# A fused Fourier mix on one core: the order of all work given as an explicit list, with the even row pairs moved and the first transform's sums dealt out anew

**Chip, cores, metric.** The kernel runs on one core of one Trainium2 chip. The metric is the device time of one execution in microseconds (us). PE is TensorE, PEld its weight loads, DVE is VectorE, ACT is ScalarE, POOL is GpSimd, SP is the engine whose queue issues nearly all transfers.

## The reference

```python
# x: 1 x 2048 x 1024 bf16; w_r, w_i: 2048 x 513; gate_w: 1024
g = sigmoid((x * gate_w).sum(-1, keepdims=True))
a = irfft2(rfft2(x) * (A_w_r + 1j * A_w_i))     # -> bf16
b = irfft2(rfft2(x) * (B_w_r + 1j * B_w_i))     # -> bf16, the same x
return g * a + (1 - g) * b
```

The transforms are computed as matrix products. The kernel has five parts, and the text uses these names for them.

- **Head.** The first transform, F1, of the 16 row groups of x. Each row gives two results, an even one and an odd one (e = 0 and 1), and each of the 32 results needs one sum and one difference of halves, a *row fold*. A row fold is done by DVE (from PSUM, after ACT has copied one half out), by POOL (from SBUF, after the whole has been copied out), or inside the matmuls (a *sum*, with twice the matmuls and then one plain copy).
- **Steps 0 to 15.** Each takes the second transform (F2, F3), multiplies by the weights W (two DVE *products*, c1 and c2, per step), does the first inverse transform, and writes a block of 512 KB to DRAM. Steps 0 to 7 belong to the even half, 8 to 15 to the odd half. In steps 0 to 7, POOL also computes three tiny *edge terms*, which the inverse matmuls need.
- **Read-backs.** The blocks return in another layout, eight row pairs for each half. An odd row pair needs the last block.
- **Row pairs.** The second inverse transform with the gate, for eight even pairs and eight odd ones. The odd ones combine both halves into the output.
- **Gate.** Two sigmoids on ACT and the gate weights on DVE. Every row pair needs its gate weights first.

## The kernel before

Its order is the order of the calls. POOL had five double folds (10 of the 32 row folds), DVE 20, and two were summed in PE.

```python
    def f1_pool(i, e, k=None):          # two rows: copied whole to SBUF by ACT, folded by POOL
        at = wk.tile([P, 2, 2, 256], F32, name="at4", tag=f"p{(i + e) % 2}", bufs=3)
        ...
        av = at[:].rearrange("p s h (a c) -> p h s a c", c=4)
        fold(nc.gpsimd, 2 * i, e, av[:, 0], av[:, 1])          # an add and a subtract
    ...
    def cmul(n, r, tts=((0, 2),)):      # one product: 128x2048 bf16, both inputs in SBUF
        ...
            nc.vector.tensor_tensor(o, xr, wv, ALU.mult)
    ...
    Wh = const.tile([P, NU, 2, 2, 4], F32, name="wh")
    for b, op in ((0, ALU.add), (2, ALU.subtract)):
        for t in range(2):
            nc.gpsimd.tensor_tensor(Wh[:, :, :, t, b:b + 2], ws[:, 0, :, :, t, b:b + 2], ws[:, 1, :, :, t, b:b + 2], op)   # waits for the small load ws
    gwz = const.tile([P, 8, 32], BF16, name="gwz")
    nc.gpsimd.memset(gwz[:], 0.0)                                                         # ACT's first work waits for this
    ...
    f1_fold(0, 0, 0)()                  # the head
    f1_pool(0, 1)
    f1_fold(2, 0, 1)()
    f1_pool(1, 1)
    ...                                 # f1_pool(4, 0), f1_pool(2, 1), f1_pool(3, 1) among DVE folds
    for n in range(3, 16):
        mid(n)                          # f3(n-1), cmul_2(n-2), load_w(n+3), f2(n), cmul_1(n-1), i1(n-2); for n = 11..14 two even read-backs
    f3(15); cmul_2(14); gate_z(0, 0); cmul_1(15); cmul_2(15)     # (one call to a line)
    i1(14, "ADA"); gate_weights(0); i1(15, "ADA")
    for s0 in range(0, NS1, 2):
        read_back(1, s0)
    i2(0, 0); gate_z(1, 0); gate_weights(1); i2(0, 1); i3_even(0, 1)
    stage = [(0, 1), (0, 2), (0, 3), (0, 4), (1, 0), (0, 5), (1, 1), (0, 6), (1, 2), (0, 7), (1, 3), ...]   # (0, v) even, (1, v) odd
```

## Time and profile before

| | |
|---|---|
| median, range of 3 runs | 125.18 us, 123.96 to 125.72 |
| span of the profiled run | 124.5 us (that run took 126.41 us) |
| busy: PE, DVE, ACT, POOL | 83%, 74%, 73%, 34% |
| POOL's folds | 10.28 to 22.68 us |
| step 3's first product | 36.5 us |
| last product of step 15 | 77.7 us |
| last block issued, landed | 82.25, 89.40 us |

In the list of instructions in order of time, the columns are the start (us), the time taken (us), the engine, the source line, the operation, what it writes and reads, how many, and in brackets how long the engine had been idle and who released it. POOL's last folds and first edge terms, in the kernel before:

```profile
20.18 2.50 POOL L257 TENSOR_TENSOR y<-at_403 128x512 bf16<-128x512 f32 x2
22.63 0.67 POOL L415 TENSOR_TENSOR e_529<-X_157,wh 128x16 f32<-128x16 bf16 x1
```

POOL is nearly through with its folds (22.68 us) when the first product needs DVE (22.08 us). The two products of step 3:

```profile
36.52 1.23 DVE L407 TENSOR_TENSOR p_779<-X_158,w_119 128x2048 bf16<-128x2048 bf16 x1 [0.48 <-ACT X_158 L384]
...
38.34 1.21 DVE L407 TENSOR_TENSOR p_780<-X_158,w_119 128x2048 bf16<-128x2048 bf16 x1
```

A run is labelled slow when it is over 1.5% above the fastest of the same kernel, and the profiled run of the kernel before was such a run.

### The profile page before, as it was taken

The page shows a single profiled execution, that of the slowest core. Times are in us where ns is not written, and L with a number is a line of the kernel's source. Part 1 is how long each engine was busy: PE and PEld are TensorE (multiplying, and loading weights), DVE is VectorE, ACT ScalarE, POOL GpSimd, SP SyncE. Part 2 cuts the span into 40 slices and gives each one's busy share as a digit, 9 for nine tenths or more (in the row PEclk, how much of TensorE's full clock was granted, in tenths as well). Part 3 has the DMA queues.
Part 4 walks back from the last instruction along what each step waited for, and adds up shares of the span by engine and source line. Part 5 has one row for each costly group of instructions (what it writes and reads, how often), then busy time and mean ns, then how long its engine had stood idle before and what let it go on. Part 6 is the DMA issues. An engine that isn't in the chain of part 4 may idle for free.

```text
span 124.5 us, 3756 instructions
## 1 busy us (share of the span) xinstructions
PE 103.7 (83%) x1556; PEld 70.9 (57%) x1558; DVE 92.5 (74%) x134; ACT 90.7 (73%) x147; POOL 42.6 (34%) x52
## 2 busy tenths in 40 slices
PE   6938999993999889988998994679919999999930
PEld 2538997872444444554454452379818999766500
DVE  0118995989689999699899899844960667778980
ACT  3029787976499999899999997699813988833510
POOL 0036999950124453400000000000000079997080
PEclk9999999999599999999999999999995999999998
DMA  2999999981929999979999999999199950407984
GB/s 93 361 396 404 384 408 411 392 328 68 290 89 308 328 294 366 316 243 239 341 402 402 413 403 412 397 399 371 55 311 419 411 213 5 169 5 286 396 335 163
DMA packets 18289, 37.41 MB, mean 301 GB/s; under 512 B 1756, under 2 KB 10848, under 8 KB 18272
## 3 DMA queue, kind: packets, MB, share of 16 engines
q1 hardware_dynamic: 17664, 36.90, 80.7%
q10 hardware_dynamic: 576, 0.26, 0.8%
q8 instruction: 12, 0.20, 0.6%
q14 instruction: 5, 0.04, 0.1%
q0 software_dynamic: 32, 0.01, 0.0%
HBM read 24.58 MB, written 12.58 MB: 299 GB/s over the span
## 4 chain that ended last, share of the span: by engine, by line
PE 29%; DVE 19%; DMA 13%; POOL 13%; ACT 13%; issue 9%; ACTq 1%; DVEq 1%; POOLq 0%
POOL y L257 10%; PE ps L454 9%; DMA h_152<-rl 6%; ACT rl L252 5%; DMA ws<-in_ws_dram 5%; DVE rl L252 4%; PE ia L436 4%; DMA ro<-h_152 3%; ACT T L252 2%; DVE y L257 2%; PE ps L353 2%; ACT X_158 L384 2%; ACT X_157 L384 2%; PE ps L313 2%; PE pt_2282 L499 1%
## 5 line engine op out<-in xcount | busy, mean ns | idle before, releaser
L465 POOL TENSOR_TENSOR ot<-re,y 128x1024 bf16<-128x1024 f32 x6 | 14.0, 2369 | 48.3 <-DVE y L465 48.3
L252 ACT CAST y<-ps 128x512 bf16<-128x512 f32 x32 | 17.5, 604 | 8.0 <-PE ps L454 8.0
L252 ACT CAST rl<-ia 128x1024 bf16<-128x1024 f32 x16 | 16.5, 1033 | 3.5 <-PE ib L436 3.4
L248 PEld LDWEIGHTS <-re 128*128 128x128 bf16 x240 | 13.6, 98 | 4.0 <-DMA re<-in_x_dram 2.2
L353 PE MATMUL ps<-fd,y 128*128 128x256 bf16 x112 | 15.4, 277 | 0.6 <-DVE e_991 L371 0.4
L252 ACT CAST T<-ps 128x512 bf16<-128x512 f32 x23 | 13.4, 635 | 0.1
L436 PEld LDWEIGHTS <-wi 32*64 32x64 bf16 x512 | 6.9, 106 | 10.4 <-issue 5.9
L353 PEld LDWEIGHTS <-y 128*128 128x128 bf16 x112 | 9.8, 98 | 4.9 <-issue 3.9
L252 DVE CAST rl<-ib 128x512 bf16<-128x512 f32 x16 | 10.9, 684 | 1.8 <-PE ib L436 1.6
L454 PE MATMUL ps<-ea,ro 128*128 128x128 bf16 x64 | 8.8, 230 | 2.8 <-DMA ro<-h_152 2.8
L454 PEld LDWEIGHTS <-ro 128*128 128x128 bf16 x128 | 8.5, 103 | 3.9 <-DMA ro<-h_152 3.1
L382 PEld LDWEIGHTS <-wf 64*64 64x64 bf16 x180 | 5.2, 108 | 9.6 <-issue 5.6
L252 ACT CAST rl<-ib 128x512 bf16<-128x512 f32 x16 | 9.8, 614 | 0.0
L475 PEld LDWEIGHTS <-y 128*128 128x128 bf16 x88 | 8.5, 102 | 1.1
L454 PE MATMUL ps<-eb,ro 128*128 128x128 bf16 x64 | 8.8, 230 | 0.0
L454 PEld LDWEIGHTS <-re 128*128 128x128 bf16 x128 | 7.8, 98 | 1.4 <-issue 1.2
L454 PE MATMUL ps<-ea,re 128*128 128x128 bf16 x64 | 8.1, 219 | 0.6 <-ACT y L252 0.6
L454 PE MATMUL ps<-eb,re 128*128 128x128 bf16 x64 | 8.1, 219 | 0.0
L248 PE MATMUL ps<-f_89,re 128*128 128x128 bf16 x96 | 6.4, 219 | 1.6 <-ACT at_180 L280 1.6
L465 DVE TENSOR_TENSOR re<-pt_2008,e_2017 128x512 f32<-128x512 f32 x2 | 1.3, 686 | 5.0 <-ACT e_2017 L479 5.0
L252 DVE CAST T<-ps 128x512 bf16<-128x512 f32 x5 | 3.4, 685 | 0.9 <-PE ps L353 0.9
L234 ACT ACTIVATE junk<-gwz 128x8 f32<-128x8 bf16 x1 | 0.2, 209 | 5.1 <-POOL gwz L231 5.1
(294 smaller groups left out, 265.2 us busy)
## 6 DMA issues: line engine op xcount, KB each, us to landing
h_151<-rl SPq DMA_DIRECT2D x8, 512.0 KB, 4.9
h_152<-rl SPq DMA_DIRECT2D x8, 512.0 KB, 8.8
re<-h_151 SPq DMA_DIRECT2D x8, 512.0 KB, 9.9
ro<-h_152 SPq DMA_DIRECT2D x8, 512.0 KB, 6.5
re<-in_x_dram SPq DMA_DIRECT2D x6, 512.0 KB, 7.1
out_dram<-ot SPq DMA_DIRECT2D x6, 512.0 KB, 2.7
ro<-in_we_dram SPq DMA_DIRECT2D x4, 512.0 KB, 7.2
ro<-in_wo_dram SPq DMA_DIRECT2D x4, 512.0 KB, 6.9
```

Source lines behind the costliest of these rows:

```text
L248: nc.tensor.matmul(o[:, q * 128:(q + 1) * 128], lhsT=x[:, s1, h * 512 + q * 128:h * 512 + (q + 1) * 128], rhs=F1[:, h * e, :], start=(h == ...
L252: (nc.scalar.copy if eng == "A" else nc.vector.tensor_copy)(out=out, in_=in_)
L257: eng.tensor_tensor(o, av, bv, op)
L313: nc.tensor.matmul(ps[32 * j:32 * j + 32], lhsT=gwz[:, k, :], rhs=y[:, k // 4, k % 4, 8 * j:8 * j + 8, :, :].rearrange("p t s c -> p (t s ...
L353: nc.tensor.matmul(ps[:, q // 2 * 256:q // 2 * 256 + 256], lhsT=y[:, par, q, 2 * t:2 * t + 2, :, :].rearrange("p j s c -> p (j s c)"), rhs ...
L382: nc.tensor.matmul(ps[hp(jh ^ tt), tt * 512 + dst:tt * 512 + dst + ln], lhsT=WF[hp(jh), 2 * u + tt, w, :], rhs=T[hp(jh), tt, src:src + ln] ...
L384: nc.scalar.copy(out=X[:].rearrange("p (r t m) -> p t r m", r=2, t=2), in_=ps[:].rearrange("p (t r m) -> p t r m", t=2, r=2))
L436: nc.tensor.matmul(bank[g][hp(tt)], lhsT=WI[h, 2 * u + tt, w, :], rhs=p[h, 4 * tt + row:4 * tt + row + 2, o:o + 256], start=(k == 0), stop ...
L454: nc.tensor.matmul(ps[:, ch * 128:ch * 128 + 128], lhsT=RR[par][:, s1, c0 + 256 * ab:c0 + 256 * ab + 128], rhs=Ew[:, s1, :], start=(ab == ...
L465: (nc.vector if engs[k] == "D" else nc.gpsimd).tensor_tensor(o[:, :, k], a, b, op)
L475: nc.tensor.matmul(ps[:, o:o + 256], lhsT=V[:, s, 2 * r + a, :], rhs=rhs[:, 2 * r + a, 0:256], start=(a == 0), stop=(a == 1))
L499: nc.tensor.matmul(ps[:, s * 512:(s + 1) * 512], lhsT=V[:, s, ch, :], rhs=IO[:, ch, :], start=(ch == 0), stop=(ch == 3))
```

## The change

Its intent: instead of calls, a list of words states the order of everything. With that freedom it zeroes gwz first and forms wh later (the small loads leave the head), deals out F1 anew, spreads the loads of W, and moves even row pairs and gate work ahead of steps 14 and 15 and all other even pairs ahead of the first odd one.

```diff
+F1_GROUPS = """            # name, kind, first row, e, rows, PSUM
+0 fold 0 0 2 1             # fold: DVE. pool: POOL. sum: matmuls
+1 pool 0 1 1 s
+3 pool 1 1 1 0
+2 pool 2 0 2 1
+4 pool 2 1 1 s
...
+8 pool 8 0 1 s
+10 pool 10 0 2 0
+12 sum 4 1 1 s
...
+18 pool 8 1 2 1            # the odd rows 8 to 15: before, six DVE folds and two PE sums
+19 pool 10 1 2 1
+20 pool 12 1 1 s
+21 sum 13 1 1 s
+22 pool 14 1 2 0
+"""
+PLAN = """
...
+f1 6; f1+ 3; f1 7; f1> 6 A; f1> 1 A; f1+ 1; f1+ 5; f1+ 6; f1> 7 D; f1 12; f1+ 4; f1 8; f1 9; f1+ 7; f1> 8 A; f1 10
...
+f2 12 1; rb 0 2; i1> 9 2 D; f3 11 w; i1> 9 1 A; f2 12 0; hb 9; i1 10 0; f3> 11 w A; c2 10 w; i1 10 1; f2> 12 0 A
...
+f2> 15 1 A; gw 0; i1 13 1; hb 12; i1> 13 0 A; c1 14 w; i1> 13 1 A; i1> 13 2 D; f3 15 w; hb 13; i2 0 1; f3> 15 w A
+gw 1; c2 14 w; i2 0 0; i1 14 0; c1 15 w; i1 14 1; i1> 14 0 A; i1> 14 2 A; i1> 14 1 D; c2 15 w; gz 1 0; i2 0 2; gz> 1
+i1 15 0; i1 15 1; i1> 15 0 A; hb 14; i1> 15 1 D; i1> 15 2 D; hb 15; i2 0 3; gw 2; rb 1 0; rb 1 4; gw 3; ev 2 0; rb 1 2
...
+"""
-    Wh = ... ; gwz memset                # wh first, then gwz
+    gwz memset; Wh = ...                 # gwz first, wh where the list says "ws"
-    f1_fold(0, 0, 0)()
-    ...                                  # all calls of the body
+    for line in PLAN.strip().splitlines():
+        for word in line.split(";"):
+            op, *args = word.split()
+            ops[op](*args)
```

In the words, `f1`, `f1>` and `f1+` are the matmuls, the copy out and the fold of a group; `c1`, `c2` the products; `ce` the edge terms; `i1`, `i1>`, `hb` the inverse matmuls, their evictions and the store of a block; `rb` a read-back; `i2`, `ev` an even row pair and its fold; `gz`, `gw` the gate; `lw` a load of W. POOL now has 18 of the 32 row folds.

## The prediction

> **What bounds the kernel now.** I read the 40 slices first, then the chain of waits from 80 us on, then the ordered lists of instructions of PE, ACT, DVE and POOL for the head (0 to 36 us) and the end (68 to 124.5 us). The page's slices show three regimes.
>
> ```profile
> PE   6938999993999889988998994679919999999930
> ...
> DVE  0118995989689999699899899844960667778980
> ACT  3029787976499999899999997699813988833510
> POOL 0036999950124453400000000000000079997080
> PEclk9999999999599999999999999999995999999998
> DMA  2999999981929999979999999999199950407984
> ```
>
> One slice is 3.11 us. From about 37 to 77 us DVE and ACT are both full: the sixteen pipeline steps run at about 3.2 us each, close to what DVE alone needs for one (two products of 1.135 us start to start, one eviction of 0.60, 0.085 of edge terms, a third of another eviction: 3.15). The edges are different. Two half-clock slices (the 5s of PEclk) each follow a hole of PE: 2.1 us at 28, 2.8 us at 90. And DMA is full from 60 to 87 us, just when the last written block must be out. The chain shows what that costs:
>
> ```profile
> 80.74 1.50 ACT rl L252 x2
> 82.24 0.02 issue
> 82.25 7.15 DMA h_152<-rl
> 89.40 0.02 issue
> 89.42 3.52 DMA ro<-h_152
> 92.94 0.05 issue
> 92.99 1.89 PE ps L454 x16
> ```
>
> The last block h_152 is issued at 82.25 and needs 7.15 us, though the same 512 KB elsewhere lands in 3.1 to 3.5 us (the shortest of h_151 and of h_152). Only then may the odd half be read back, 3.52 us. I call 92.94 the barrier. From there PE works without a hole until the last two row pairs begin at 115.82; after that come 8.7 us of last products, DVE and stores.
>
> In the head, the first eviction waits for a small load: POOL forms wh from ws (7.32 to 8.26), then zeroes gwz; ACT's table-warming instruction waits for gwz and runs at 8.54, though its table is loaded at 3.4 and PE has finished its first tile near 5.
>
> **What the skill says.** The Trainium skill, "GPSIMD Engine Reference", section 1 Specifications, says that GpSimd's SBUF interfaces are shared with VectorE, with contention when a DVE instruction has two SBUF inputs. The product of this kernel (X times w) has two. The trace agrees:
>
> ```profile
> 21.41 1.27 POOL L257 TENSOR_TENSOR y<-at_403 128x512 bf16<-128x512 f32 x1
> 22.08 1.76 DVE L407 TENSOR_TENSOR p_525<-X_157,w_116 128x1024 bf16<-128x1024 bf16 x2 [1.03 <-ACT X_157 L395]
> ...
> 43.38 1.22 DVE L407 TENSOR_TENSOR p_941<-X_158,ro 128x2048 bf16<-128x2048 bf16 x1
> 43.47 1.22 POOL L418 TENSOR_TENSOR p_941<-e_944,e_910 128x8 bf16<-128x8 f32 x1
> ```
>
> An eight-element POOL operation that takes 0.23 us elsewhere takes 1.22 behind a product. The other way, the first half product at 22.08 took 1.14 us against 0.70 for the second, because POOL's fold ended at 22.68. So the two take turns, whole instructions at a time. DVE's own folds read one operand from PSUM; POOL's folds stay at 1.24 us beside them. "TensorE: Matmul & The Clock Gate", Part 1, says that the array falls to half clock after an idle window of about 3.4 us; here 2.1 us and 2.8 us of hole were enough, and 93 to 96 us ran at 0.50. "DMA: Bandwidth & Descriptors", section "Issuing engines are not separate DMA queues", says that all transfers share the 16 engines; the 7.15 us against 3.5 us shows it.
>
> **The change part by part.** The arithmetic stays; every engine gets a new order.
>
> *End.* (1) All eight even read-backs now follow h_151's last block, and the last stands before block 11 (of 0 to 15) instead of behind block 12; all W loads stand before block 7 (before: behind block 9). After that only the 512 KB blocks are left, one per 3.2 us, so I expect 3.7 us instead of 7.15 for the last: 3.4 us saved. (2) All eight even row pairs stand before the first odd one, three of them before step 15's products (before: three behind the barrier). The barrier-to-115.82 stretch was 11 row-pair groups x 0.89 + 7 folds x 0.87 + 3 odd x 1.73 = 21.1 us, measured 22.8 because the first group and fold ran at half clock. Now it is 8 x 0.89 + 7 x 0.87 + 3 x 1.73 = 18.4: 2.7 us less. (3) Even work left after step 15's products is 5 x 0.89 + 4 x 0.87 = 7.9 us against 1 + 3.7 + 3.5 = 8.2 us until the barrier, so PE has no hole long enough for the half clock: 1.6 us saved. (4) The odd read-backs now come 0, 4, 2, ...; the second row pair used is third to land: about 0.5 us lost. Net 7.2 us, counted from the moment the last block is issued.
>
> *Head.* gwz is zeroed first, so the first eviction can run near 5.5 instead of 8.66. But the loads of x are as before (last one about 14.8), and the folds are dealt out anew. POOL had five double groups, 5 x 2.48 = 12.4 us. It now has five doubles and eight singles. From 1.24 us for 512 elements and about 0.2 us for tiny ones I estimate 0.68 us for 256, so 1.37 per single: 23.4 us in all, 11 us more. DVE loses four double folds (4 x 1.2) and gets ten evictions (about 6.6 us). ACT gets lighter.
>
> POOL's first fold needs x rows 2 and 3 (7.08), 24 matmuls and a 1024-wide eviction: 9.65. In POOL's order the group of row 8, which every first F2 matmul needs, is sixth: 9.65 + 2.48 + 3 x 1.37 + 2.48 + 1.37 = 20.1. So F2 begins at 20.1 against 18.79 before, although PE and ACT are ready by 17.5. Products begin near 24.7 (22.08 before). From there POOL still has 18 (1 double), 19 and 22 (doubles), 20 (single) and three sets of edge terms: 3 x 2.48 + 1.37 + 3 x 0.6 = 10.6 us, and must take turns with six products of 1.135 us. DVE also waits in line: its eviction of group 20 reuses the product buffer of step 0, so it waits for step 0's inverse matmuls, which wait for POOL's edge terms; step 2's product waits for POOL's fold of 20, and step 3's for the fold of 22. Stepping through these turns one by one I get step 3's first product at 41; without any taking of turns POOL ends at 34 and it would start at 35.5. Before it started at 36.52. I take 40: 3.5 us lost.
>
> *Middle.* From step 3's first product DVE must still do 26 x 1.135 + 16 evictions x 0.60 + 4 x 0.60 + 0.3 + 4 gate operations x 0.45 = 43.7 us until the last block is issued. Before it was 41.5 of work in 82.25 - 36.52 = 45.7 us. With ACT, PE and W ahead I allow 1.5 us of idleness: 45.2. The last block goes at 40 + 45.2 = 85.2 instead of 82.25: 3 us lost.
>
> *Sum.* 85.2 + 3.7 + 3.5 = 92.4 for the barrier, + 0.5 + 18.4 + 8.7 = 120.0 against a span of 124.5. The profiled run took 126.41 us for that span, and the median was 125.18, so 1.9 us comes on top and the usual run is 1.2 shorter: 120.7.
>
> **The rivals.** *A: POOL hides.* If folds and products overlap, or a single fold is cheaper than 1.37 us, step 3 starts at 35.5 to 36, the last block goes near 81, and the time is 116 to 117. For it: POOL idled after 27 us in the old kernel, and an explicit list was presumably made so that each engine just fits. Against it: the exclusion in the four lines above. *B: the head eats the end.* Step 3 at 42 and the old 4.2 us of idleness in the middle put the last block at 42 + 43.7 + 4.2 = 90; the end saves 7.2, and the time is about 125. For it: nothing in the middle can catch up, as DVE is near its floor. Against it: after POOL's last fold ACT, the W loads and PE stand ready, so DVE should run densely. *C: the write stays slow.* If the late middle pushes read-backs and W loads into the last blocks again, the 3.4 us of (1) go, and 124 results. Against it: the eight even read-backs have no block behind them but five, 2.6 MB, which at 400 GB/s is 6.5 us of 16.
>
> **Range and chances.** Two terms matter: the start of step 3 (35.5 to 42) and the idleness behind it (1 to 4). Both good gives 116, both bad about 125; 80 in 100 lie between 116.5 and 124. The 2% mark is 122.7; I give 0.72 to faster, 0.21 to within 2% and 0.07 to slower.
>
> **What would show it.** The profile after should show: the first ACT eviction at about 5.5; POOL without a hole from 9.7 to near 40, with folds of 256 elements at 0.68 and some folds stretched beside products; F2 at 20; step 3's first product at 40; the last h_152 block issued at 85 and landed in under 4.5 us; no half-clock slice after the barrier; and 18.4 us of PE from there to the last two row pairs. It is wrong if POOL ends its folds before 35, if the last block still takes 7 us, or if DVE's idleness from step 3 on stays over 3 us.

## The result

The changed kernel is correct and slower: 131.62 us median (130.42 to 131.65, four runs) against 125.45 us (123.96 to 125.83, four runs) in the same rounds. The ratio of the fast runs is 1.051, with a 95% interval of 1.039 to 1.063. Ratios in this document are the mean time of one kernel's fast runs over the mean of the other's fast runs in the same rounds, so they are not quite the ratio of the medians that stand beside them. The prediction of 120.7 us, range 116.5 to 124, was wrong.

The slices of the changed kernel (one is 3.2 us):

```profile
PE   6999858986823998998899889589797899999700
...
DVE  0488981399697589979989998977847468799850
...
POOL 1039999999999054570000000000000019999450
PEclk9999996899998699999999999999999999999995
DMA  3999999990599389999956999999519992009992
```

POOL is full until 42 us; before, it was until 25. Beside it PE falls to 2 and 3 from 35 to 42 us, and the clock is lowered at 39 to 45 us and also at 19 to 26. At the other end there is no lowered clock after the barrier, as predicted. At 64 to 71 us, where DMA was full before, it has a hole.

The list of instructions shows what POOL's longer share does to DVE and what DVE does to POOL:

```profile
23.98 2.55 POOL L312 TENSOR_TENSOR y<-at_466 128x512 bf16<-128x512 f32 x2
24.81 2.27 DVE L483 TENSOR_TENSOR p_510<-X_150,w_116 128x1024 bf16<-128x1024 bf16 x1 [1.40 <-ACT X_150 L307]
28.86 1.21 DVE L483 TENSOR_TENSOR p_588<-X_151,w_117 128x2048 bf16<-128x2048 bf16 x1
28.87 3.55 POOL L312 TENSOR_TENSOR y<-at_563 128x512 bf16<-128x512 f32 x2
...
35.24 3.47 POOL L312 TENSOR_TENSOR y<-at_617 128x512 bf16<-128x512 f32 x2
35.31 2.28 DVE L483 TENSOR_TENSOR p_746<-X_150,w_118 128x2048 bf16<-128x2048 bf16 x1 [1.03 <-POOL y L312]
```

The first half product arrives at 24.81, while the first operation of a double fold runs on POOL, and takes 2.27 us instead of 0.70: it waits for the second operation too. At 28.86 the product comes first, by 10 ns, and the pair of operations takes 3.55 us instead of 2.5. At 35.31 a whole product waits for one fold operation only and takes 2.28 us instead of 1.21; the second operation is held behind it, and the pair takes 3.47 us.

Then the chain of waits from 33.7 to 41.7 us runs along POOL, and what follows on DVE:

```profile
33.93 4.79 POOL y L312 x4
38.72 1.16 POOL e_765 L493
...
39.95 1.10 POOL p_746 L496
...
41.10 0.63 PE ia L514 x2
```

```profile
39.72 1.23 DVE L483 TENSOR_TENSOR p_790<-X_151,w_119 128x2048 bf16<-128x2048 bf16 x1
43.27 0.17 DVE L451 TENSOR_TENSOR e_836<-ps,wh 128x16 f32<-128x16 f32 x1 [2.32 <-issue]
...
43.96 1.21 DVE L483 TENSOR_TENSOR p_791<-X_151,w_119 128x2048 bf16<-128x2048 bf16 x1
```

POOL is done with the edge term p_746 of step 2 at 41.05, because three row folds (a single and a double one) stood ahead of it. PE's inverse matmuls of step 2 wait for it. In PE's order the small matmul of step 3 (it starts at 42.96) stands behind them, and DVE, in its own order, waits for that matmul for 2.32 us. So step 3's second product starts 4.2 us after its first. In the kernel before it was 1.8 us. The profile puts DVE's wait down to "issue"; the chain names POOL.

Near the end of the steps, the chain of the changed kernel is this:

```profile
72.37 11.55 DMA re<-h_144
...
83.96 1.07 PE ps L543 x16
...
90.42 4.74 DMA h_145<-rl
...
95.18 0.33 SPq L374
```

An even read-back issued at 72.37 lands 11.55 us later, and PE stands for it (rows_by_use, below, shows that little hangs on this). The inverse matmuls of step 14 are behind that row pair in PE's order. The last block leaves at 90.42 instead of 82.25; it then lands in 4.74 us instead of 7.15.

Where the time went, in us from the start of the span. The middle column is the trace of a fast run of the old order; mended is a kernel from the experiments, shown here for comparison.

| | before, profiled (long run) | before as a list (fast run) | changed | mended |
|---|---|---|---|---|
| step 3's first product | 36.5 | 36.8 | 39.7 | 35.4 |
| last block issued | 82.2 | 82.5 | 90.4 | 82.4 |
| first odd read-back issued | 89.4 | 89.1 | 95.2 | 85.6 |
| first matmul of the last two row pairs | 115.7 | 113.8 | 118.0 | 108.8 |
| span | 124.5 | 122.6 | 128.6 | 119.7 |

From the second column to the third: 2.9 lost to step 3, 5.0 more to the last block, 1.8 won to the read-back, 1.9 won to the last row pairs, 1.8 lost at the very end: 6.0 us, close to the 6.2 us between the medians.

### The profile page after: what moved, and what is told of

The parts are those of the page before. It is cut to its first block, busy times and chain, and to the rows that moved or that the text cites.

```text
span 128.6 us, 3755 instructions
## 1 busy us (share of the span) xinstructions
PE 105.8 (82%) x1558; PEld 70.6 (55%) x1558; DVE 97.8 (76%) x137; ACT 87.1 (68%) x136; POOL 57.1 (44%) x68
## 4 chain that ended last, share of the span: by engine, by line
PE 30%; DMA 17%; ACT 8%; DVE 8%; POOL 6%; issue 4%; SPq 1%; DVEq 1%; ACTq 0%; POOLq 0%
DMA re<-h_144 9%; PE ia L514 6%; PE ps L543 5%; PE ps L425 5%; DMA ro<-h_145 4%; ACT rl L307 4%; POOL y L312 4%; DMA h_145<-rl 4%; ACT T L307 2%; PE ps L386 1%; PE pt_2329 L588 1%; PE pt_2245 L588 1%; PE pt_2295 L588 1%; SPq L374 1%; DVE ot L593 1%
## 5 line engine op out<-in xcount | busy, mean ns | idle before, releaser
L425 PE MATMUL ps<-fd,y 128*128 128x256 bf16 x112 | 16.9, 281 | 4.8 <-DVE e_775 L451 2.3
L425 PEld LDWEIGHTS <-y 128*128 128x128 bf16 x128 | 11.4, 102 | 12.9 <-issue 9.1
L303 PEld LDWEIGHTS <-re 128*128 128x128 bf16 x240 | 14.8, 103 | 2.2 <-DMA re<-in_x_dram 1.4
L543 PEld LDWEIGHTS <-re 128*128 128x128 bf16 x128 | 7.6, 98 | 3.4 <-DMA re<-h_144 1.7
L543 PE MATMUL ps<-ea,ro 128*128 128x128 bf16 x64 | 8.0, 219 | 1.5 <-DMA ro<-h_145 1.5
L543 PEld LDWEIGHTS <-ro 128*128 128x128 bf16 x128 | 7.7, 98 | 2.8 <-DMA ro<-h_145 2.1
L307 ACT CAST rl<-ib 128x512 bf16<-128x512 f32 x15 | 9.0, 605 | 0.0
L564 PEld LDWEIGHTS <-y 128*128 128x128 bf16 x88 | 8.2, 98 | 0.8
L543 PE MATMUL ps<-eb,ro 128*128 128x128 bf16 x64 | 8.0, 219 | 0.0
L303 PE MATMUL ps<-f_89,re 128*128 128x128 bf16 x56 | 4.2, 220 | 0.5 <-DVE e_586 L451 0.5
L483 DVE TENSOR_TENSOR p_510<-X_150,w_116 128x1024 bf16<-128x1024 bf16 x2 | 2.9, 1487 | 1.4 <-ACT X_150 L307 1.4
L368 POOL TENSOR_TENSOR wh<-ws 128x32 f32<-128x32 bf16 x4 | 0.9, 269 | 6.6 <-DMA ws<-in_ws_dram 6.6
```

Of the source, the lines that this page charges most:

```text
L303: nc.tensor.matmul(o[:, q * 128:(q + 1) * 128], lhsT=x[:, s1, h * 512 + q * 128:h * 512 + (q + 1) * 128], rhs=F1[:, h * e, :], start=(h == ...
L307: (nc.scalar.copy if eng == "A" else nc.vector.tensor_copy)(out=out, in_=in_)
L425: nc.tensor.matmul(ps[:, i * 512 + q // 2 * 256:i * 512 + q // 2 * 256 + 256], lhsT=y[:, par, q, 4 * u + 2 * t:4 * u + 2 * t + 2, :, :].re ...
L543: nc.tensor.matmul(ps[:, ch * 128:ch * 128 + 128], lhsT=RR[par][:, s1, c0 + 256 * ab:c0 + 256 * ab + 128], rhs=Ew[:, s1, :], start=(ab == ...
L564: nc.tensor.matmul(ps[:, o:o + 256], lhsT=V[:, s, 2 * r + a, :], rhs=rhs[:, 2 * r + a, 0:256], start=(a == 0), stop=(a == 1))
```

## The experiments

Each kernel is the old or the new list with a few words moved. The old order, written as a list, gives the same order of instructions on all five engines; the two traces show the same. All results were correct.

| kernel | median us | before, same rounds | ratio of fast runs (95%) |
|---|---|---|---|
| changed | 131.62 | 125.45 | 1.051 (1.039 to 1.063) |
| headA_restB: new head, old rest | 131.31 | 125.12 | 1.056 (1.048 to 1.065) |
| headB_restA: old head, new rest | 126.15 | 125.12 | none (one fast run) |
| rows_by_use | 130.73 | 125.12 | 1.051 (1.041 to 1.060) |
| rows_unblocked | 131.15 | 125.12 | 1.050 (1.038 to 1.063) |
| less_on_pool | 125.31 | 123.94 | 1.014 (1.008 to 1.020) |
| edges_on_dve | 131.94 | 123.94 | 1.067 (1.060 to 1.075) |
| small_loads | 122.86 | 123.94 | 0.993 (0.989 to 0.998) |
| headB_unblocked | 123.05 | 123.94 | 0.992 (0.982 to 1.001) |
| fold_behind_edge | 131.58 | 125.88 | 1.056 (1.030 to 1.082) |
| evens_last | 134.24 | 125.88 | 1.087 (1.075 to 1.099) |
| combo | 122.68 | 125.88 | 0.990 (0.974 to 1.006) |
| combo_evens_last | 125.91 | 125.88 | none (too few fast runs) |
| more_on_pool | 130.67 | 125.97 | 1.055 (1.047 to 1.064) |
| even_folds_first | 123.75 | 125.97 | 1.000 (0.992 to 1.007) |
| repaired ("mended" above) | 122.48 | 125.97 | 0.988 (0.982 to 0.993) |
| combo_again | 121.98 | 125.97 | 0.984 (0.976 to 0.991) |
| before_as_list | 125.40 | 124.36 | 1.014 (1.006 to 1.021) |

### Which half loses: headA_restB and headB_restA

```diff
 headA_restB: the changed list up to F2 of step 3, the first product of step 2 and step 1's block; from there the words of the kernel before
 headB_restA: the head of the kernel before; from step 3 on the changed list
```

> The changed order up to step 2 (all column transforms, the new split of the folds, gwz first), then the old order from step 3 on. Theory HEAD (eight single folds on POOL, which take turns with DVE's products, delay step 3 and nothing behind can catch up): step 3's first product at 39 to 40.5 us, the whole 2.5 to 4 us slower than the kernel before, ratio 1.02 to 1.035. Rival TAIL (the head is absorbed by slack later; the loss is made by the new order of read-backs and even row pairs): ratio within 0.99 to 1.01.

> The old order up to step 2, then the changed order. HEAD: step 3's first product back at 36 to 37, about 3 us faster than the changed kernel, which leaves 1.015 to 1.03 of the kernel before (the rest has its own net loss of about 1 to 3 us). TAIL alone: as slow as the changed kernel, 1.045 to 1.055.

The new head with the old rest was as slow as the whole change (1.056), worse than theory HEAD had said (1.02 to 1.035). The old head with the new rest had a median of 126.15 us against 125.12, and its one fast run, 123.60 us, is no better than the fast runs of before (123.58 to 125.28); step 3's first product came at 38.5 us in its profiled slow run, not at the 36 to 37 expected. So the head alone makes the loss, and the new order of the rest shows no gain as it stands. The chain of waits of headA_restB begins like this:

```profile
9.69 14.35 POOL y L311 x18
...
24.21 2.52 POOL y L311 x2
26.74 0.65 POOL e L501
...
34.77 4.16 POOL y L311 x3
38.92 1.16 POOL e L501
```

From 9.7 to 41 us the end of the kernel hangs on POOL alone.

### The order of the even read-backs: rows_by_use and rows_unblocked

```diff
 rows_by_use: the eight rb words keep their places
-rb 0 14 | rb 0 4 | rb 0 6 | rb 0 2 | rb 0 12 | rb 0 8 | rb 0 0 | rb 0 10
+rb 0 2 | rb 0 0 | rb 0 4 | rb 0 6 | rb 0 10 | rb 0 14 | rb 0 8 | rb 0 12
 rows_unblocked: the new order, two read-backs each behind hb 8, hb 9, hb 10 and hb 11
```

> The changed kernel, but the eight even read-backs in the order in which the row pairs use them (2, 0, 4, 6, 10, 14, 8, 12 instead of 14, 4, 6, 2, 12, 8, 0, 10); their places in the queue are the same. If PE's wait for the read-back of row 2 (1.55 us at 82 us, in front of step 14's products) is what delays the last block, the wait is gone, the last block goes 1 to 1.5 us earlier and the whole is 1 to 1.5 us faster than the changed kernel (ratio to before 1.035 to 1.045). If the wait only stood beside DVE's work, no change: 1.045 to 1.055.

> As rows_by_use, and each pair of even read-backs one block later, so that the queue issues block 8 before it waits for block 7 to land. In the changed kernel the queue stood 5.3 us in that wait and the DMA engines ran at 124 GB/s from 65 to 70 us. If this hole is what leaves too much traffic for the end, the last block lands in under 4 us (4.7 in the changed kernel), the DMA rate from 65 to 70 is over 250 GB/s, and the whole is a further 0.5 to 1.5 us faster. If the traffic of the end comes from the late middle as a whole, no change against rows_by_use.

Neither changed the time clearly. In rows_by_use PE's wait of 1.55 us was gone, and yet the last block went out 50.5 us after step 3's first product, against 50.7 in the changed kernel: that wait had only stood beside DVE's work. In the changed kernel, SP's queue stands from 62.35 to 67.81 us, waiting for the eighth block to land before the first read-back:

```profile
61.99 0.36 SPq L529 DMA_DIRECT2D h_144<-rl  x1
67.81 0.81 SPq L374 DMA_DIRECT2D re<-h_144  x2
```

In rows_unblocked another block went out in that time, but the first read-back still started at 67.62 us, because what it waits for is the landing, and the eighth block was issued no earlier. As long as the head is late, nothing is gained here.

### GpSimd's share: less_on_pool, edges_on_dve, fold_behind_edge, more_on_pool

```diff
 less_on_pool
-18 pool 8 1 2 1
+18 fold 8 1 2 1
-19 pool 10 1 2 1
+19 sum 10 1 2 1
-20 pool 12 1 1 s
+20 sum 12 1 1 s
-22 pool 14 1 2 0
+22 sum 14 1 2 0
-f1> 18 D; ... f1+ 18            # DVE copies 18 whole, POOL folds it
+f1> 18 A; f1+ 18                # ACT copies half, DVE folds it in the place of the copy
```

> The changed kernel, but the last four groups of the first transform that it gave to GpSimd (7 of GpSimd's 18 row folds) leave GpSimd: one becomes a VectorE fold in the place where VectorE had copied it, three are summed by the matmuls, evicted by the engines that evicted them. VectorE keeps its time, TensorE gets some 5 us more. Theory GPSIMD (the chain of waits of the run with the changed head lies on GpSimd's folds from 9.7 to 41.3 us; the split of the sums gave it too much): GpSimd is done by about 28 instead of 42 us, step 3's first product starts at 36 to 37 us as before instead of 39.7, no half-clock slices at 30 to 45 us, and the time falls from 131.6 to 125 to 127 us, 0.95 to 0.97 of the changed kernel. Rival ORDER (the head loses by the order in which TensorE and VectorE get their work, whoever folds): it stays at 130 to 132 us.

The ratio fell from 1.051 to 1.014. POOL's last fold ended at 24.7 us instead of 38.7, and no slice had a lowered clock before the last one. The first half product met an idle POOL:

```profile
22.59 2.11 POOL L311 TENSOR_TENSOR y<-at 128x256 bf16<-128x256 f32 x3
24.94 0.69 DVE L491 TENSOR_TENSOR p<-X,w 128x1024 bf16<-128x1024 bf16 x1 [1.39 <-POOL y L311]
```

Step 3's first product came at 38.2 us, later than the 36 to 37 that I had expected, but the second followed at 40.1 without the stall. This is the largest single cause, shown by taking it away: 3.7% of the time of before (by the medians, of different rounds, 6.3 us). PE even has 40 more matmuls in this kernel than in the changed one.

```diff
 edges_on_dve, in the edge terms
+        eng = nc.vector if n < 3 else nc.gpsimd
-        nc.gpsimd.tensor_tensor(e1[:], xs, Wh[:, n], ALU.mult)
+        eng.tensor_tensor(e1[:], xs, Wh[:, n], ALU.mult)          # and the two that follow
```

> The changed kernel with the edge terms of steps 0, 1 and 2 (three small operations each) on VectorE instead of GpSimd, where they stand behind folds. All folds stay on GpSimd. Theory GPSIMD QUEUE (the loss comes only from the edge terms' place behind the folds: TensorE waits for them until 41 us): the wait of 2.3 us on VectorE at 41 us goes, the time falls by 2 to 4 us to 128 to 129.5. Rival GPSIMD FOLDS (the folds themselves are late, because the last of them feed the sums that the odd steps and the gate need, and they stretch VectorE's products by taking turns with them): under 1.5 us of gain, 130 us or more.

It came out no better (1.067), so nothing speaks for the theory that only the edge terms' place counts. But the experiment also brought a wait that I had not foreseen, because with the edge terms gone POOL's folds follow each other without a gap; so it does not measure the place of the edge terms alone. First DVE, then POOL, in this run:

```profile
24.48 6.14 DVE L491 TENSOR_TENSOR p<-X,w 128x1024 bf16<-128x1024 bf16 x1 [1.39 <-ACT X L306]
```

```profile
23.06 7.01 POOL L311 TENSOR_TENSOR y<-at 128x256 bf16<-128x256 f32 x7
```

A half product of 0.69 us took 6.14. It stood until 30.62, half a microsecond after POOL's last fold in line had ended at 30.07. Of the seven fold operations on the POOL line, one was running when it came, and four more started and ended before it. So this product did not take the next turn; it waited until the line was empty. That is not a rule: in the same run a whole product that came at 39.62 took 1.80 us, while the second operation of POOL's pair was held behind it and took 2.25 us instead of 1.27, and the product at 35.31 in the changed kernel took the next turn as well. In the nine traces in which fold operations went ahead of a waiting product, it was the first half product each time; why, I have not found out.

```diff
 fold_behind_edge
-f1> 18 D; ... c1 0 0; f1+ 18; c1 0 1; ... ce 0
+f1> 18 D; ... c1 0 0; c1 0 1; ... ce 0; f1+ 18
```

> The changed kernel with one GpSimd fold pair (the two odd rows 8 and 9) moved behind the edge terms of step 0 in GpSimd's order, so that its queue is empty when VectorE's first half product arrives. In the changed kernel that half product took 2.27 us, in the other runs with GpSimd's 18 folds 3.70, 3.72, 3.71 and 6.14 us, each time until GpSimd's folds in line were through; where GpSimd had finished its folds it took 0.7 us. Theory LOAD (what counts is the sum of GpSimd's folds and VectorE's products, which take turns, up to 41 us): the half product takes 0.7 us, but step 3's first product still starts at 39 to 40.5 us and the time is within 1 us of the changed kernel. Rival HELD PRODUCT (the one product held behind folds is the loss): step 3 starts 2 us earlier, the time falls to 129 us or less.

The half product took 0.69 us, as theory LOAD had it, and the kernel gained nothing: 131.58 us median, step 3's first product at 41.5 us. Its profiled run was a slow one, so the start of step 3 is not comparable to a microsecond; that it came no earlier is enough. The one held product is not the loss; theory LOAD, by which the sum of POOL's folds and DVE's products is, fits.

```diff
 more_on_pool: the kernel before as a list
-b13 fold 8 1 2 1
+b13 pool 8 1 2 1
-b14 sum 10 1 2 1
+b14 pool 10 1 2 1
+f1+ b14                    # behind its copy: a sum needed no fold
-b15 fold 12 1 1 s
+b15 pool 12 1 1 s
-b17 fold 14 1 2 0
+b17 pool 14 1 2 0
```

> The kernel before, written as a list, in its own order, with 7 more row folds on GpSimd (the odd rows 8 to 12, 14 and 15: two folds and a single one of VectorE and one sum of TensorE become GpSimd's); GpSimd gets 17 rows in place of 10, VectorE and TensorE get less. Theory LOAD (GpSimd's share is the cause, whatever the order): GpSimd's folds last until about 38 to 40 us, step 3's first product starts at 39 to 40 instead of 36.5 us, the time is 1.02 to 1.05 of before. Rival ORDER (it costs only with the changed order): 0.99 to 1.01.

The old order with 17 instead of 10 row folds on POOL needed 1.055 of before, and step 3's first product came at 42.2 us, worse than expected. Nothing else of the change is in this kernel. So POOL's share makes a loss of this size by itself, in either order. Where it comes out depends on the order: here it lies wholly before step 3, and from step 3's first product to the last block it took 45.8 us, as in the kernel before (45.7).

### The other end: headB_unblocked, evens_last, combo, combo_evens_last

```diff
 headB_unblocked: headB_restA with the read-backs of rows_unblocked
```

> The head of the kernel before (with its split of the sums), the order of the changed kernel for the rest, and the even read-backs in order of use, each pair issued one block later than in the changed kernel, so that the store queue does not stand for a block that has not landed. In the run with the old head and the changed rest, TensorE waited until 80.3 us for an even row (10.9 us from issue to landing), step 14's inverse products stood behind it, and the last block left at 86.8 instead of 82.3 us. Theory READ-BACK (that wait eats the drain's gain): the last block leaves by 84 us, the time falls to 121 to 123 us, 0.97 to 0.985 of before. Rival DMA (the transfers in the drain fill all queues whatever the order): 124 to 126 us, as before.

0.992, with 1.001 as the upper end of the interval. Theory READ-BACK had said 121 to 123 us and 0.97 to 0.985, so the median of 123.05 us stands at its edge and the ratio shows that it was too hopeful. The last block was issued at 84.6 us, and the odd read-back at 87.89 instead of 91.43.

```diff
 evens_last
-hb 13; i2 0 1; ... gw 1; c2 14 w; i2 0 0; i1 14 0; ... c2 15 w; gz 1 0; i2 0 2; gz> 1; i1 15 0; ... hb 15; i2 0 3
+hb 13; ... c2 14 w; i1 14 0; ... c2 15 w; i1 15 0; ... hb 15; i2 0 1; i2 0 0; gz 1 0; gz> 1; gw 1; i2 0 2; i2 0 3
```

> The changed kernel with the three even row pairs, the second half of the gate and its weights, that it had moved ahead of the inverse products of steps 14 and 15, behind them. Its last products start 3.7 us later, counted from the kernel before, than step 13's (77.3 against 72.0 us, but 86.7 against 77.7 us). Theory DRAIN (the moved row pairs stand in TensorE's order ahead of the last steps, and wait there for read-backs): the last product starts at 83 to 84 instead of 86.7 us and the last block leaves 3 us earlier; since the same row pairs then lie between the last block and the odd read-back, where TensorE is otherwise idle, the time falls by 1 to 3 us. Rival CONSERVED (TensorE is busy nearly all the time from there on, so moving work along it changes nothing): the last block leaves earlier, but the time stays within 0.7 us.

Both theories were wrong: 1.087, 2.6 us slower than the changed kernel by the medians of different rounds. The last product started at 88.0 us, no earlier, because another wait took the place of the read-back's. ACT's list in that run:

```profile
87.35 1.01 ACT L307 CAST rl<-ia 128x1024 bf16<-128x1024 f32 x1 [2.44 <-DMA h<-rl]
```

The eviction of step 14 goes into one of four buffers, rl, and the block that used it last was still on its way to DRAM behind the read-backs. And with the even pairs gone from there, PE had nothing to fill the wait (from 83 to 90 us it was busy for 3.54 of 7 us, and from 90 to 93 its clock was 0.71).

```diff
 combo: headB_unblocked with the head of small_loads
 combo_evens_last: combo with the even pairs behind step 15, as in evens_last
```

> The two changes that helped, together: the head of the kernel before with GpSimd's small weights formed after its first fold pair (0.993 of before alone), and the changed kernel's order from step 3 on with the even read-backs in order of use and one block later (0.9915 alone). If they add: 0.98 to 0.987 of before, 121.5 to 122.5 us at a before of 124. If the head's gain is taken up by the wait for the transfers later: 0.99.

> The same as combo, with the three even row pairs behind step 15's inverse products. Theory DRAIN: 1 to 3 us less than combo. Rival CONSERVED: as combo within 0.7 us.

combo had a median of 122.68 us, combo_evens_last 125.91 us in the same rounds, but that compares mostly fast runs with mostly slow ones. combo_evens_last has one fast run, 123.64 us, against a mean of 122.35 for the three of combo: 1.3 us. It points the same way as evens_last: moving even pairs ahead of the last steps, the core of the change, is better than placing those three behind. By how much isn't settled: 2.6 us in the changed kernel, from different rounds, and 1.3 us here, from one run. combo itself came to 0.990, not the 0.98 to 0.987 that adding the two gains would have given.

### The small loads: small_loads

```diff
-    wh from ws; gwz zeroed
+    gwz zeroed
-f1+ b1                     # POOL's first fold
+f1+ b1; ws                 # wh only behind it
```

> The kernel before, written as a list, with one part of the change alone: GpSimd zeroes the gate weights first and forms the symmetric small weights only after its first pair of folds, so that it does not wait for the small load of these weights at the head. My prediction counted on a head without that hole. If GpSimd's start is on the path of the kernel before (its folds end at 25 us and carry 10% of its chain of waits): 1 to 2 us less, 0.985 to 0.995 of before. If the path at 25 us is TensorE and VectorE, with GpSimd beside it: same, within 0.5%.

0.993 (0.989 to 0.998). POOL's first fold started at 7.86 instead of 10.28 us and the folds ended at 21.7 instead of 22.7. This part of the change looks like a small gain by itself: its fast runs, 122.14 to 122.90 us, all lie below those of before, from 123.17; the control below says how far so small a difference can be trusted.

### Mending the change: even_folds_first, repaired, combo_again

```diff
 even_folds_first: less_on_pool, and in POOL's order
-3; 1; 4; 10; 8; 13
+3; 8; 10; 1; 4; 13          # 8 and 10 are even rows, needed by step 0; 1 and 4 odd, needed by step 8
 repaired: even_folds_first with the read-backs of rows_unblocked
```

> The changed kernel with fewer folds on GpSimd (1.0138 of before) and, further, GpSimd's fold order changed in one point: the two folds of odd rows 0 and 2, not needed before step 8, go behind the last even-row folds, on which the second transform of step 0 waits. Theory EVEN FOLDS: step 0's first product starts 1.5 to 2 us earlier (23 instead of 24.9 us), and the time falls to 0.998 to 1.005 of before. Rival: VectorE's own even folds end at 18.7 us and the x loads vary by as much, so step 0 gains under 0.7 us and the time stays at 1.01 to 1.015.

> even_folds_first with the even read-backs in order of use and one block later. With the old head this made 0.9915 out of 1.008. If the drain's gain adds to the mended head: 0.985 to 0.995 of before, so the changed kernel's idea, mended in two places, would beat the kernel before. If not: as even_folds_first.

> combo once more with five rounds: 0.983 to 0.992 of before if its first measurement (0.99, interval 0.974 to 1.006) holds.

even_folds_first came to 1.000 (0.992 to 1.007), from 1.014; step 0's first product started at 23.6 instead of 24.9 us. Its chain of waits then hung on an even read-back, 11.43 us from issue to landing. repaired removes it and comes to 0.988 (0.982 to 0.993). The slices of repaired (3.0 us each):

```profile
PE   6999998999899979988999799999898999997800
...
POOL 1039999992153455700000000000000079999430
```

The same edit of the read-backs that did nothing in the changed kernel is worth about 1.2% here (in the same rounds, every run of repaired, up to 122.91 us, lies below every run of even_folds_first, from 123.43), where the head is no longer late. combo_again, the old split of the sums with the two helpful parts, came to 0.984 (0.976 to 0.991). Both beat the kernel before, whose fastest run in these rounds was 123.56 us, and they are within each other's intervals.

### A control: before_as_list

> The kernel before written as a list of words, with the order of instructions the same on each engine as in the kernel before. If the rewriting is neutral: 0.995 to 1.005 of before. If it costs (another allocation of buffers, other waits): over 1.01, and the experiments that start from the old order have to be read against this run and not against before.

It came out at 1.014 (1.006 to 1.021), which I had not expected, with 125.40 us against 124.36. Its trace is the kernel before's to within 0.3 us at every product up to 78.0 us but the two of step 2, which are 1.0 and 0.8 us late, and its profiled span, 122.6 us, is that of a usual run of the kernel before. In those rounds the kernel before had runs from 122.64 to 126.79 us, of which only those up to 124.4 count as fast, while the list's fast runs go up to 125.9. So either the list costs a little, or a ratio near 1.01 can come from the choice of fast runs. I can't tell which. The consequence: differences of 1% between single kernels here are not safe, those of 3 to 5% are; and measured against their own list form, more_on_pool loses 4% rather than 5.5%, and small_loads and combo_again gain more than the table says.

## Why the prediction was wrong, point by point

**What bounds the kernel now.** The reading that DVE and ACT fill the middle held, but not its sum: from step 3's first product to the last block DVE had 42.8 us of work and was idle for 2.9 us in the kernel before, where the prediction had 41.5 and 4.2. The barrier's half clock was in the one long run that had been profiled, and not in the fast run of the same order: there PE's hole was 2.29 us instead of 2.82, the clock stayed up, and the stretch took the 21.1 us of PE work that the prediction had worked out. So the 1.6 us of its part (3) were not there to save in that run, and the 1.2 us that the sum takes off again for the usual run count some of the same time twice.

**Head.** Right in mechanism and size. POOL ran without a hole to 41.8 (predicted: near 40), single folds took 0.68 us each, ACT took T at 20.61 (F2 at about 20), step 0's product came at 24.81 (24.7), step 3's at 39.72 (40). ACT's first eviction came at 6.59, not 5.5, without consequence that I saw. The Trainium skill, "GPSIMD Engine Reference", section 8 Key points, calls DVE structurally about twice as fast for elementwise work; this trace agrees: a double fold takes 2.48 us on POOL and 1.20 us on DVE (two operations, start to start).

**Middle: the step that failed.** "With ACT, PE and W ahead I allow 1.5 us of idleness: 45.2." It took 50.7 us, 5.5 more. DVE was idle for 6.0 us instead of 1.5, and its work took 44.7 us instead of 43.7. The largest piece of the idleness, 2.32 us at 41 us, is POOL's: the prediction followed POOL's lateness to step 3's first product and stopped there, as if the queue behind it were empty. The edge terms of step 2, behind the folds, still held PE, and PE's order passed the wait back to DVE. In less_on_pool, where POOL was done early, the same stretch took 47.8 us, with 3.1 us of idleness: so 2.9 of the 5.5 us go with POOL's seven folds. The other large piece is at the last steps: from step 13's second product to the last one it took 9.4 us instead of 5.7. DVE had the gate weights, 1.7 us, in front of its products. I had counted those in the work, but not the waits. PE's wait of 1.55 us for the even read-back is not what makes this piece: in rows_by_use it was gone, and these products still took 8.5 us, as they did in the mended kernel. No kernel with the new rest came near 1.5 us of idleness; the mended one had 2.7 us, and the stretch took 47.0. What makes up this remainder was not tested.

**End.** The parts were there, but smaller. The last block landed in 4.74 us, not 3.7 (the old order's fast run: 6.54). Read-back to first odd group was 3.6 us (3.5). From the barrier to the last pairs I had 18.9 us, and 118.0 - 98.8 = 19.2 came. The very end took 10.5 us instead of 8.7: the last matmuls wait for DVE to free PSUM. This was seen in the trace and not tested; the mended kernel has it too (10.9 us) and wins all the same.

**The sum.** 5.5 (middle) + 1.0 (landing) + 1.8 (end) + 0.5 (odd group, row pairs) - 0.3 (step 3 earlier than assumed) = 8.5 us, against 128.6 - 120.0 = 8.6 us of span.

**The rivals.** Rival B, the head eats the end, is what happened, and worse than it was written; it had been dismissed with "POOL's last fold ACT, the W loads and PE stand ready, so DVE should run densely". Rival A fell with the first product of 2.27 us. Rival C came true in part: the read-backs landed late and PE stood for one of them, but by rows_by_use little time hung on that.

**By experiments, in ratios to before:** the changed kernel 1.051; without 7 of POOL's 18 row folds 1.014; with the two odd folds behind the even ones 1.000; with the read-backs in order 0.988. What is left of the change then is a gain of about 1.2%. Except for the last two, these kernels were measured in different rounds, each against the kernel before in its own, and with the control in mind the small step from 1.014 to 1.000 is less sure than the first.

## What to carry to other kernels

Before giving work to an engine that looks idle, add up its whole list and the work of the engine it shares memory access with, and follow its last result past the first reader, through the order of every engine in between. When a change of many parts loses, put the old and the new half of the order together crosswise first: two runs here told that the head was to blame, and one more, with four groups dealt out differently, told which part of it. A good part can be hidden by a bad one: the order of the read-backs showed no gain until the head was mended.

## What the Trainium skill lacked or had wrong

- "SBUF — State Buffer", section "SBUF: two separate sides", says that of a DVE operation with two SBUF inputs and a GpSimd operation that reads SBUF the one that starts first holds the shared ports for the whole instruction, and the other blocks. The runs agree (POOL's pair of folds 3.55 us instead of 2.5 behind a product). What the page lacks is who is next when several are in line: a DVE half product of 0.69 us came up behind back-to-back POOL folds and took 2.27, 3.70 and 6.14 us in three runs, the last with four more fold operations started ahead of it, while whole products later in the same traces took the very next turn (2.28 us at 35.31 us). So one instruction's length is not always the bound of the wait; what decides was not found.
- "TensorE: Matmul & The Clock Gate", Part 1, gives an idle window of about 3.4 us, free-running, before the clock halves. In the runs shorter holes were enough, and the length alone does not tell: 2.08 us at 28 us was followed by a lowered clock in both traces of the old order (0.54 and 0.77 at 32 to 35 us), but a hole of 2.08 us at 31 us in headB_restA by 1.00 (33.2 to 38 us); 2.82 us at the barrier by 0.52 (92.7 to 96 us), and 2.29 us at the same place by 1.00.
- No page has the cost of a POOL operation of a few elements beside DVE products: 0.23 us alone, 1.1 to 1.26 us when a product of 1.22 us runs, and it is the next engine's inverse matmuls that wait for it.
